# Infini-attention and a dense layer on one core: tile 1's V products ahead of wk's, and the order list searched again

## The chip, the core and the metric

One Trainium2 chip, one core of it. The time is microseconds of the device for one execution of the whole program. Engines are named as in the profile: PE (matrix products), DVE (vector), ACT (activations), POOL (GpSimd), SP (the queue from which nearly all transfers are issued). PSUM is the memory into which PE writes; the kernel uses eight banks of it, 512 float32 columns each.

## What is computed

`xn` is the layer norm of `x` (2048 rows of 512, bfloat16). Two things are added to `x`:

```python
# A: 32 heads of 16, four segments of 512 rows; M and z start at 0
p = softmax(q_s @ k_s.T / 4 + mask); a_dot = p @ v_s
a_mem = (phi(q_s) @ M) / (phi(q_s) @ z + 1e-6)       # phi(t) = t + 1 if t > 0 else exp(t)
o_s = sigmoid(beta) * a_mem + (1 - sigmoid(beta)) * a_dot
M, z = M + phi(k_s).T @ v_s, z + sum(phi(k_s))
# out = x + concat(o_s) @ wo + silu(xn @ w1) @ w2      (B: w1 is 512 x 1792)
```

`mask[i, j]` is -1e9 where i < j and 0 elsewhere.

## The kernel before

The work is cut into some 1349 small pieces, each a call of a short function, and one string, `ORDER` (from line 16, one line of it for each visit), lists them in the order in which they are issued. Every engine executes its own pieces in that order and waits for the others by semaphores alone. A launcher at the end of the kernel (line 895 on) reads the string word by word; `S0`, `h0.0.1`, `vv0.0` are such words: a piece's name and its numbers.

The segments (the first number of most words, s) have 512 rows, four tiles of 128. The words that the texts below use:

- `xs t` (L291; `xc`, `xd` its halves, L286 and L289): layer norm statistics of tile t on DVE; `xg`, `xq`, `xi` the inverse root; `Nv t` (L315): the normalised rows, on DVE.
- `X t.1` (L845): four transposes of tile t on PE, for tiles 0 to 3; `Xa`, `Xv` (L851) copy the result into xnT. Tiles from 4 on are turned by a transfer of SP (`XD t`, L857).
- `k s.dt.part`, `q`, `h`, `v s.tile.part` (L370, L395, L485, L401; through `product`, whose two forms are L336 and L338): a part of a product of xn with wk, wq, w1, wv. A part is one product of 512 columns in segments 0 and 1 (for k, q and h of segment 0 two of 256), two of 512 later on; four parts, later two, fill a PSUM bank.
- `kv`, `ka`, `qv`, `qa`, `vv`, `va` (L376, L399, L406): the finished bank is copied to SBUF, by DVE (`v` behind the name) or ACT (`a`). `kp`, `kf` (L385, L392, L393) make the keys' parity copies k3 from it.
- `ha` (L492), `hv` (L497): tanh on ACT, then the product on DVE, which frees the bank of h. `fp`, `fa`, `fv` (L417, L423, L433): phi of k, on POOL, ACT and DVE; `gp`, `ga`, `gv` of q.
- `S t` (L707 to L760): a visit. PE makes scores of four heads into psS, one tile of four banks (L724), ACT exponentiates all of it (L730), POOL masks (L744). There is one psS, so that the next visit's products wait for the exponential of the one before. Each exponential also waits for its place in ACT's order.
- `E n`, `O n` (L791): weights by V, even and odd heads; `Ev`, `Ov` (`Ea`, `Oa`) copy them out (L821, L828) and two transfers move the sums into zraw; `Om` (L835) merges.
- `s`, `sv`, `r`, `w` (`R`, `W` in the last segment): sums, their reciprocals and the gate; `z`, `d` (L577): transfers that spread them, `zv`, `dv` (L589, L599) the products; `n`, `nv` (L608): the memory's part; `t` (L441), `m`, `mv`, `mw` build the memory.
- `o s.tile.i` (also `oc`, `od`, `oh`: a half, a quarter, half a row): the last product, of hT with w2 for i up to 13 and of the attention with wo for 14 to 17; `st`, `sh` add x and store.

Two things bound the freedom of the list. PSUM: four banks are psS's, and the other four go round among k, q, v, h, E, O, n, m, s, X and o; a word that opens a bank waits until the copy of the bank's last content is done. And the array: a score product takes the array in row tiles, E and O in column tiles of 32, dense words either whole (L336) or in columns (L338), whichever suits the next S, E, O, s or m in the list; the launcher decides it so:

```python
        elif piece in ("k", "q", "v", "h", "n", "o", "oc", "od", "oh"):
            now = ahead[i] if now == "rows" else now
            now = "whole" if now == "rows" else now
        narrow[0] = now == "cols"
        PIECES[piece](*(int(n) for n in word[len(piece) :].split(".") if n))
```

Which of the four banks a word gets follows from the order, too: the pool hands out one that is free at that place of the list. The loads of x and of the weights stand ahead of the list, on SP's and ACT's queues: x tiles 0 to 3, wv, wk, wq, x tiles 4 to 7 (x_hi), w1, the rest of x. 50 products on zeros (`busy`) run while the first tile is normalised.

Of the kernel before, what the change touches and what calls it, by code (L numbers as in the profile page):

```python
# [25 lines left out]
S6 fa0.3 k1.2.0 k1.2.1 k1.2.2 h0.5.0 h0.5.1 h0.5.2 q1.1.0 h0.5.3 ha0.5 k1.2.3 kv1.2 q1.1.1 q1.1.2 hv0.5
S8 h0.7.0 q1.1.3 qv1.1 h0.6.0 h0.6.1 h0.6.2 h0.6.3 ha0.6 fv0.3 E1 Ev1 k1.0.0
S9 hv0.6 h0.7.1 h0.7.2 h0.7.3 Om0 ha0.7 k1.0.1 k1.0.2 kp1.2 q1.0.0 q1.0.1 q1.0.2 fp0.1 Nv9 XD9 xs12 k1.0.3 kv1.0 kp1.0
S10 h0.8.0 hv0.7 h0.8.1 h0.8.2 h0.8.3 ha0.8 h0.9.0 h0.9.1 q1.0.3 t0.3 Nv10 XD10 h0.9.2 h0.9.3 qv1.0
S13 hv0.8 O1 Ov1 xs15 v1.0.0 v1.0.1 v1.0.2 ha0.9 v1.0.3 vv1.0 h0.10.0 h0.10.1 bmask  # L30
S12 k1.1.0 k1.1.1 k1.1.2 t0.2 k1.1.3 kv1.1 h0.10.2 h0.10.3 ha0.10 hv0.9 h1.0.0 Om1 h1.0.1 h1.0.2
S15 h1.10.0 h1.10.1 h1.10.2 hv0.10 kp1.1 xl0.2 h1.0.3 ha1.0 Nv11 XD11 E2 Ev2 O2 Ov2
S17 h1.10.3 k1.3.0 hv1.0 k1.3.1 k1.3.2 k1.3.3 kv1.3 fp1.3 h0.12.0 h0.12.1 xs14 m0.2 mv0.2 ha1.10 h0.12.2
S21 fv0.1 q1.3.0 q1.3.1 q1.3.2 q1.3.3 qv1.3 h1.3.0 hv1.10 gp1.1 h0.12.3 ha0.12 t0.1 h1.3.1 h1.3.2 t0.0 h1.3.3
S14 hv0.12 k2.2.0 h0.11.0 h0.11.1 k2.2.1 h0.11.2 h0.11.3 xl0.0 h0.13.0 ha1.3
S16 ha0.11 h0.13.1 h0.13.2 kp1.3 h0.13.3 xs13 kv2.2 hv1.3 ha0.13 q2.1.0 q2.1.1 qv2.1 E3
S19 Ev3 h1.11.0 h1.11.1 h1.11.2 h1.11.3 hv0.11 O3 hv0.13 fa1.3 k2.1.0 mw0.2 k2.1.1 Ov3 kv2.1 Om2
S24 h1.8.0 h1.8.1 h1.8.2 h1.8.3 m0.0 mv0.0 q2.3.0 q2.3.1 qv2.3 ha1.8 hv1.8
S18 v2.1.0 v2.1.1 vv2.1 ga1.0 k2.0.0 o0.2.7 oc0.2.5.0 ha1.11 sv0 r0.1 o0.2.4 k2.0.1 kv2.0 xg12.4
S22 fv1.3 v2.2.0 v2.2.1 vv2.2 o0.2.1 ga1.1 gp1.2 o0.2.6 o0.0.3 o0.0.13 od0.2.11.1 hv1.11 r0.2 o0.0.10  # L40
S20 o0.2.0 oc0.0.2.0 r0.3 lw1 o0.2.2 od0.0.0.2 oc0.2.10.1 h1.1.0 h1.1.1 h1.1.2 h1.1.3 kp2.1 E4 r0.0 od0.0.0.1 ha1.1 gate w0 gv1.1 kp2.0 z0.1
S28 o0.0.6 hv1.1 z0.2 o0.0.8 z0.3 o0.0.11 o0.0.5 Ev4 oc0.0.7.1 Om3 z0.0 o0.2.8 o0.0.12 ga1.2 O4 Ov4
S26 q2.0.0 q2.0.1 h1.7.0 h1.7.1 h1.7.2 h1.7.3 gv1.2 ha1.7 qv2.0 oc0.2.10.0 od0.0.0.3 oc0.0.2.1
S23 fp1.2 od0.2.11.3 h1.4.0 hv1.7 h1.4.1 h1.4.2 Nv14 o0.2.12 h1.4.3 ha1.4 od0.2.11.0 oc0.0.7.0 zv0.3 h1.9.0 o0.2.13 h1.9.1
S25 h1.9.2 h1.9.3 ha1.9 Nv12 XD12 o0.2.3 oc0.2.5.1 gp1.0 zv0.2 o0.2.16 o0.0.16 hv1.4 zv0.0 XD14 zv0.1 E5 o0.0.17 Ev5 hv1.9
S29 fa1.2 o0.2.17 o0.2.14 k2.3.0 gv1.0 k2.3.1 kv2.3 h1.2.0 h1.2.1 h1.2.2
S27 o0.0.9 mw0.0 O5 o0.2.15 Ov5 o0.2.9 Nv13 fp1.0 XD13 h1.2.3 ha1.2 od0.2.11.2 fv1.2 st0.2 t1.2 o0.0.14 o0.0.15
S31 o0.0.4 h1.13.0 h1.13.1 h1.13.2 h1.13.3 ha1.13 o0.3.8 Om5 o0.3.11 o0.3.16 hv1.2 o0.3.9
S30 o0.3.14 h1.12.0 h1.12.1 h1.12.2 h1.12.3 t1.3 Nv15 hv1.13 ha1.12 XD15 od0.0.0.0 o0.1.16 od0.1.8.2 o0.1.17 o0.1.12 hv1.12 oc0.1.9.0
S33 o0.0.1 od0.1.8.3 o0.3.1 xl0.1 od0.1.8.0 st0.0 oc0.1.3.0 o0.1.13 oc0.1.3.1 xl0.3 gp1.3 Om4 fa1.0 o0.1.2 E6 o0.1.0  # L50
S32 kp2.3 Ev6 O6 Ov6 o0.3.17 o0.3.13 o0.3.10 o0.1.6 oc0.3.2.1 o0.1.15 m1.2 fa2.0 mv1.2 fv1.0
S35 o0.1.4 q2.2.0 q2.2.1 qv2.2 fp2.0 ga1.3 v2.0.0 v2.0.1
S34 h1.5.0 h1.5.1 o0.1.14 o0.1.11 t1.0 vv2.0 h1.5.2 oc0.3.0.1 xl1.0 gv1.3 fp1.1 h1.5.3 ha1.5 E7
S41 o0.1.7 Ev7 o0.3.12 o0.1.1 hv1.5 O7 v2.3.0 mw1.2 fa1.1 Ov7 v2.3.1 vv2.3 fv1.1 t1.1
S37 o0.3.5 q3.3.0 q3.3.1 Om7 qv3.3 od0.1.8.1 s1 o0.1.5 sv1 r1.2 o0.1.10 oc0.1.9.1 st0.1 r1.0 od0.3.3.2 ga2.3 kp2.2
S36 k3.1.0 k3.1.1 q3.1.0 q3.1.1 qv3.1 r1.3 r1.1 w1 d1.2 z1.1 z1.2 ka3.1 o0.3.4
S40 h1.6.0 h1.6.1 h1.6.2 h1.6.3 fp2.3 h2.8.0 h2.8.1 ha1.6 o0.3.7
S43 oc0.3.0.0 o0.3.6 od0.3.3.0 hv1.6 od0.3.3.1 m1.0 mv1.0 oc0.3.2.0 od0.3.3.3 o0.3.15 st0.3 o1.2.8 ha2.8 o1.2.7 hv2.8 fv2.0 E8 Ev8 gp2.3
S38 o1.2.13 fa2.2 v3.0.0 v3.0.1 Om6 k3.0.0 od1.2.1.1 k3.0.1
S42 kv3.0 o1.2.6 o1.2.2 o1.2.10 d1.1 h2.11.0 h2.11.1 ha2.11 o1.2.0 t2.0 vv3.0 zv1.1 gv2.3 o1.2.4 fp2.2 zv1.2  # L60
S39 hv2.11 q3.2.0 ga2.1 q3.2.1 qv3.2 d1.0 v3.3.0 v3.3.1 va3.3 E9
S44 dv1.2 q3.0.0 q3.0.1 Ev9 mw1.0 oc1.2.3.1 oc1.2.11.1 od1.2.1.3 fv2.2 gp2.2 n1.2 d1.3 O8 nv1.2 fa2.3 Ov8 xl1.2 oc1.2.3.0
S45 oc1.2.11.0 o1.2.9 h2.7.0 h2.7.1 ha2.7 qv3.0 fv2.3 v3.2.0 v3.2.1 vv3.2
S48 hv2.7 h2.6.0 h2.6.1 ha2.6 k3.2.0 k3.2.1 z1.3 dv1.3 o1.0.4 dv1.0 kv3.2 ga2.2 o1.0.0 oc1.0.7.1
S47 od1.0.1.3 hv2.6 h2.0.0 od1.2.1.2 h2.0.1 ha2.0 dv1.1 zv1.3 t2.2 n1.3 Om8 o1.0.6 o1.2.5 o1.0.16 nv1.3 hv2.0 gp2.1 o1.0.13
# [877 lines left out]
```

## Time and profile before

| what | value |
|---|---|
| three runs | 220.78, 219.94, 220.15 us; median 220.15 |
| the profiled execution | 219.96 us, of which its span is 218.2 us |
| PE, ACT, DVE, POOL busy | 210.9, 184.1, 181.3, 127.4 us |
| granted clock of PE | 1.00 |
| exponentials | 72, 1.88 us each, the first at 12.4, the last at 190.4 us |
| wk's load | issued at 2.68, on the chain that ended last for 5.81 us |
| last product on PE | starts at 215.0 us |

A line of the timeline gives the start, the duration, the engine, the line of the code, the operation and the tiles (out<-in); in square brackets stands the time that the engine stood idle before it, and what ended that. "x10" says that ten instructions in a row were merged. The windows give each engine's busy time in a stretch. Where a busy engine is named as the bound, its pace has to be looked at, since a busy PE can be one that waits inside.

### The profile page before, as it was taken

To read this page: it belongs to the slowest core of one execution; us is meant where nothing else is said; L and a number is where in the kernel's file an instruction comes from. 1 tells how busy PE (TensorE), PEld (TensorE's weight loads), DVE (VectorE), ACT (ScalarE), POOL (GpSimd) and SP (SyncE) were. 2 spreads that over 40 slices of the span, in tenths; PEclk is the share of its full clock that TensorE was granted. 3 is DMA by queue.
4 is the path that set the end of the run, shared out by engine and by line. 5 is a ranking of instruction groups with operands and counts; after the bars stand their busy time and mean duration, and the time that the engine had idled before them with its cause. 6 is when DMAs were issued, how large, how long until landed. Compare 5 with 4: busy or idle time off the path is not lost.

```text
span 218.2 us, 9267 instructions
## 1 busy us (share of the span) xinstructions
PE 210.9 (97%) x3982; PEld 116.1 (53%) x4006; DVE 181.3 (83%) x370; ACT 184.1 (84%) x173; POOL 127.4 (58%) x203
## 2 busy tenths in 40 slices
...
PEclk9999999999999999999999999999999999999999
...
DMA packets 33273, 19.60 MB, mean 90 GB/s; under 512 B 14672, under 2 KB 33232, under 8 KB 33232
## 3 DMA queue, kind: packets, MB, share of 16 engines
...
q8 instruction: 31, 0.51, 1.0%
...
## 4 chain that ended last, share of the span: by engine, by line
PE 92%; DMA 3%; ACT 2%; issue 1%; SPq 1%; DVE 0%
PE ps L336 26%; PE psO L338 17%; PE ps L338 16%; PE psS L724 11%; PE psO L336 9%; PE psV L791 8%; PE psS L338 4%; DMA wk_sb<-in_A_wk_dram 3%; ACT Pb L730 2%; PE psM L452 1%; SPq L169 0%; SPq L158 0%; PE ps L509 0%; ACT th L492 0%; DVE o_half L668 0%
## 5 line engine op out<-in xcount | busy, mean ns | idle before, releaser
L730 ACT ACTIVATE Pb<-psS 128x2048 bf16<-128x2048 f32 x72 | 135.2, 1878 | 4.7 <-PE psS L724 2.4
L744 POOL TENSOR_SCALAR_AFFINE_SELECT Pb<-Pb 128x512 bf16<-128x512 bf16 (+2 forms) x88 | 62.3, 718 | 22.4 <-ACT Pb L730 19.6
L497 DVE SCALAR_TENSOR_TENSOR hT<-th,ps 128x512 bf16<-128x512 bf16 x56 | 38.0, 682 | 10.1 <-ACT th L492 9.4
L744 POOL TENSOR_SCALAR_AFFINE_SELECT lows<-Pb 64x512 bf16<-64x512 bf16 (+1 forms) x40 | 24.3, 607 | 32.0 <-ACT Pb L730 24.9
L338 PE MATMUL psO<-w_sb,hT 128*32 128x512 bf16 (+2 forms) x696 | 41.4, 321 | 0.0
L336 PE MATMUL ps<-xnT,w_sb 128*128 128x512 bf16 (+1 forms) x177 | 35.9, 330 | 0.2 <-issue 0.2
L492 ACT ACTIVATE th<-ps 128x512 bf16<-128x512 f32 x56 | 33.0, 594 | 3.5 <-PE ps L338 3.1
L338 PEld LDWEIGHTS <-hT 128*32 128x32 bf16 x864 | 21.5, 96 | 14.6 <-issue 3.1
L338 PE MATMUL ps<-xnT,w_sb 128*32 128x512 bf16 (+1 forms) x408 | 24.8, 349 | 0.0
L724 PE MATMUL psS<-qT,k 32*128 32x64 bf16 (+3 forms) x512 | 23.0, 233 | 0.2
L336 PEld LDWEIGHTS <-w_sb 128*128 128x128 bf16 x178 | 16.4, 98 | 11.9 <-issue 1.2
L336 PE MATMUL psO<-w_sb,hT 128*128 128x512 bf16 (+2 forms) x82 | 20.5, 324 | 0.7 <-issue 0.6
L791 PEld LDWEIGHTS <-Vz 128*32 128x32 bf16 x768 | 16.1, 97 | 9.5 <-issue 0.6
L791 PE MATMUL psV<-Pb,Vz 128*32 128x448 bf16 (+7 forms) x512 | 21.0, 286 | 0.0
L724 PEld LDWEIGHTS <-k 32*128 32x128 bf16 x512 | 9.3, 92 | 21.2 <-issue 20.4
L336 PE MATMUL ps<-xnT,wk_sb 128*128 128x256 bf16 (+1 forms) x63 | 14.4, 326 | 0.4 <-DMA wk_sb<-in_A_wk_dram 0.2
L724 PE MATMUL psS<-qT,kT 16*128 16x448 bf16 (+3 forms) x256 | 14.7, 269 | 0.0
L338 PEld LDWEIGHTS <-w_sb 128*32 128x32 bf16 x408 | 10.3, 96 | 6.7 <-issue 1.7
L621 DVE SCALAR_TENSOR_TENSOR o_out<-psO,x_res 128x512 bf16<-128x512 f32 x14 | 9.4, 679 | 5.0 <-PE psO L338 3.9
L336 PEld LDWEIGHTS <-hT 128*128 128x128 bf16 x92 | 8.5, 98 | 9.6 <-issue 2.1
L828 DVE CAST odd<-psV 128x512 bf16<-128x512 f32 x16 | 11.0, 687 | 2.4 <-PE psV L791 2.4
L338 PE MATMUL psO<-wo_sb,oT 128*32 128x512 bf16 x140 | 12.8, 379 | 0.0
...
## 6 DMA issues: line engine op xcount, KB each, us to landing
...
```

Source lines behind the costliest of these rows:

```text
L336: return [nc.tensor.matmul(out, lhsT=lhsT, rhs=rhs, start=start, stop=stop, skip_group_check=True)]
L338: nc.tensor.matmul(out[c : c + 32], lhsT=lhsT[:, c : c + 32], rhs=rhs, start=start, stop=stop, tile_position=(0, c), skip_group_check=True,)
L452: nc.tensor.matmul(psM[32 * g : 32 * g + 32, i, :].rearrange("p (r d) -> p r d", d=DH), lhsT=st["phiK", dt][:, j, 32 * g : 32 * g + 32], r ...
L492: nc.scalar.activation(out=th[:], in_=sts[s]["h", ft][:, :], func=AF.Tanh, scale=0.5)
L497: nc.vector.scalar_tensor_tensor(out=st["hT"][:, ft, :], in0=st.pop(("th", ft))[:], scalar=1.0, in1=st.pop(("h", ft))[:, :], op0=ALU.add, ...
L621: out = nc.vector.scalar_tensor_tensor(out=o_out[:], in0=st.pop(("psO", j)), scalar=0.5, in1=st["x", j][:], op0=ALU.mult, op1=ALU.add)
L724: nc.tensor.matmul(psS[:, g, c : c + q2 - q1], lhsT=keys[rows], rhs=st["qT"][rows, dt, q1:q2], start=True, stop=True, tile_position=(32 * ...
L730: exp = nc.scalar.activation(out=blocks(Pb, b).rearrange("p y g c -> p g y c"), in_=psS[:, :, :].rearrange("p g (y c) -> p g y c", c=BLOCK ...
L744: over[id(Pb)].append(nc.gpsimd.affine_select(out=out, in_=in_, compare_op=ALU.is_ge, fill=0.0, base=base, pattern=[[0, out.shape[1]], [1, ...
L791: nc.tensor.matmul(psV[32 * g : 32 * g + 32, q0 : q0 + nq].rearrange("p (y c) -> p y c", y=weights.shape[2]), lhsT=Vzs[s % 2][:, kt, 4 * d ...
L828: copy(out=odd[:], in_=sts[s].pop(("psV", 1))[:, :])
```

## The change

Nothing but the string `ORDER` is changed. The set of pieces is the same but for nine copies, which go to the other of DVE and ACT. Ahead of S0, wk's product k0.1.0 gives its place, between the transposes X2 and X3, to v0.1.0, and v0.1.1 follows X3; words of the dense products around the first visits stand earlier or later; and from there on the whole list has another order, the order of the visits excepted. From the diff, the head, the first visits, and the lines that the prediction names:

```diff
-ones0 ones1 zeros xc0 xd0 xc1 xq0 xi0 Nv0 busy44 xd1 xq1 xc2 busy6 xi1 X0.1 xd2 xq2 Nv1 X1.1 Xa0.1 v0.0.0 v0.0.1 v0.0.2 xs3 xi2 Nv2 xq3 xi3 v0.0.3 X2.1 Xa1.1 k0.1.0 tb Nv3 X3.1 Xv2.1 k0.1.1 Xv3.1 vv0.0 odd omask k0.0.0 k0.0.1 k0.0.2 k0.0.3 ka0.0 fp0.0 q0.0.0 kf0.0 q0.0.1 q0.0.2 q0.0.3 k0.1.2 k0.1.3 q0.2.0 v0.2.0 qa0.0 xs5 ka0.1 kp0.1
-S0 v0.1.0 v0.1.1 xs6 xs7 q0.2.1 v0.2.1 v0.2.2 v0.2.3 vv0.2 fa0.0 k0.2.0 k0.2.1 k0.2.2 xs4 xg4.4
-S2 q0.2.2 q0.2.3 qv0.2 k0.2.3 kv0.2 fp0.2 fa0.2 v0.1.2 v0.1.3 vv0.1 Nv5 Nv6 XD6 q0.1.0 q0.1.1 q0.1.2 q0.1.3 qv0.1
-S1 h0.0.0 h0.0.1 h0.0.2 xs10 h0.0.3 v0.3.0 v0.3.1 v0.3.2 v0.3.3 ha0.0 vv0.3 q0.3.0 kp0.2 hv0.0
-S3 h0.3.0 h0.3.1 q0.3.1 q0.3.2 h0.3.2 tanh XD5 h0.3.3 k0.3.0 Nv7 XD7 q0.3.3 qv0.3 k0.3.1 xs8 ha0.3
-S4 Nv4 h0.1.0 k0.3.2 h0.1.1 hv0.3 XD4 h0.2.0 h0.2.1 h0.2.2 h0.2.3 ha0.2 xs9 k0.3.3 kv0.3 hv0.2
...
+ones0 ones1 zeros xc0 xd0 xc1 xq0 xi0 Nv0 busy44 busy6 X0.1 xd1 xq1 xc2 xi1 xd2 xq2 Nv1 X1.1 Xa0.1 v0.0.0 v0.0.1 xs3 v0.0.2 xi2 Nv2 v0.0.3 xq3 xi3 Nv3 Xa1.1 X2.1 Xv2.1 v0.1.0 X3.1 Xv3.1 v0.1.1 tb k0.0.0 k0.0.1 vv0.0 k0.0.2 odd k0.0.3 ka0.0 kf0.0 fp0.0 k0.1.0 xs5 q0.0.0 q0.0.1 q0.0.2 q0.0.3 qa0.0 k0.1.1 k0.1.2 k0.1.3 kv0.1 kp0.1 xs7 fa0.0
+S0 xs4 v0.2.0 v0.2.1 v0.2.2 v0.2.3 v0.1.2 xs6 xg4.4 k0.2.0 k0.2.1 va0.2 k0.2.2 k0.2.3 kv0.2 fp0.2
+S2 q0.1.0 q0.1.1 v0.1.3 vv0.1 fa0.2 q0.1.2 q0.1.3 qv0.1 q0.2.0 q0.2.1 q0.2.2 q0.2.3 qv0.2
+S1 q0.3.0 q0.3.1 Nv6 XD6 h0.0.0 Nv7 h0.0.1 h0.0.2 h0.3.0 h0.0.3 h0.2.0 ha0.0 fv0.2 xs9 hv0.0 q0.3.2
+S3 h0.3.1 h0.3.2 h0.2.1 h0.2.2 h0.3.3 ha0.3 Nv5 q0.3.3 fp0.1 tanh qv0.3 k0.3.0 k0.3.1
+S4 k0.3.2 k0.3.3 hv0.3 v0.3.0 XD7 kv0.3 kp0.3 v0.3.1 Nv4 h0.2.3 ha0.2 h0.1.0 v0.3.2 v0.3.3 vv0.3 h0.1.1
+S7 kp0.2 xs11 h0.1.2 h0.1.3 ha0.1 XD5 v1.2.0 v1.2.1 v1.2.2 v1.2.3 XD4 E0 hv0.2
+S5 v1.1.0 v1.1.1 v1.1.2 v1.1.3 vv1.2 Ev0 xl0.2 h0.4.0 h0.4.1 h0.4.2 h0.4.3 ha0.4 h0.5.0 hv0.1 xs8 xs10 hv0.4 xg8.4
+S11 v1.3.0 v1.3.1 h0.5.1 h0.5.2 omask vv1.1 h0.5.3 v1.3.2 v1.3.3 vv1.3 O0 Ov0 fa0.1 lw0
+S6 ha0.5 fv0.1 q1.2.0 q1.2.1 q1.2.2 q1.2.3 fa0.3 Nv9 Nv10 k1.2.0 k1.2.1 qv1.2 q1.1.0 q1.1.1 q1.1.2 q1.1.3 XD9 qv1.1
+S8 XD10 h0.6.0 h0.6.1 h0.6.2 h0.6.3 hv0.5 fp0.3 xs13 k1.2.2 k1.2.3 kv1.2 ha0.6 h0.8.0 h0.8.1 E1 Ev1
...
+S16 h0.13.1 h0.13.2 h0.13.3 Om2 ha0.11 q2.1.0 q2.1.1 t0.0 Nv12 kp1.2 qv2.1 E3 Ev3 ha0.13 hv0.13
+S19 Om0 Nv14 XD14 h1.11.0 h1.11.1 h1.11.2 h1.11.3 ha1.11 O3 Ov3 q2.3.0 kp1.3 q2.3.1 hv0.11 qv2.3
+S24 h1.8.0 hv1.11 gate h1.8.1 h1.8.2 h1.8.3 ha1.8 k2.1.0 k2.1.1 o0.2.7 kv2.1 kp2.1
...
+S46 hv2.0 oc1.0.10.0 h2.12.0 o1.0.0 zv1.0 d1.1 dv1.1 h2.12.1 ha2.12 O9 dv1.0 o1.2.17 Ov9
...
+S62 d2.3 o2.0.7 od2.0.6.2 o2.0.8 o2.2.3 n2.0 nv2.0 xl2.2 o2.0.11 z2.1 od2.2.13.2 zv2.3 oc2.2.6.0 o2.0.9 ga3.0 E13 Ev13 gv3.1
+S63 h3.4.0 h3.4.1 ha3.4 o2.2.10 O13 oc2.0.5.1 Om9 o2.2.12 mw2.0
+S67 Ov13 oc2.2.6.1 hv3.4 o2.2.0 o2.2.2 h3.8.0 dv2.3 gv3.0 h3.8.1 ha3.8 n2.3 nv2.3 o2.2.5 o2.2.14
...
+S65 o2.1.13 od2.1.9.2 o2.1.15 Om12 o2.1.2 o2.0.4 d2.2 dv2.2 o2.1.7 oc2.0.5.0 E14 Ea14 oc2.1.3.0 o2.0.15
...
```

The last line of the list, S71, holds in both kernels what is left of the output products, with the last segment's R, W, z, d and n between.

121 lines of the change are left out of this document (54 added, 67 removed).

## The prediction

> **What bounds the kernel now.** I read the page first, then the windows, the matrix products (PE) in the timeline, and the list word by word. The first two lines are the page's, the next the clock; below them the tile view's exponentials and five stretches of the windows (columns: PE, PEld, DVE, ACT, POOL busy, clock, DMA share, GB/s).
>
> ```profile
> span 218.2 us, 9267 instructions
> PE 210.9 (97%) x3982; PEld 116.1 (53%) x4006; DVE 181.3 (83%) x370; ACT 184.1 (84%) x173; POOL 127.4 (58%) x203
> PEclk9999999999999999999999999999999999999999
> ...
> L730 ACT ACTIVATE Pb<-psS x72: 1872/1877/1898, 12.4 to 190.4; 128x2048 bf16<-128x2048 f32 x72
> ...
> 0.00:10.00 10.00, 8.09 (x81) 6.87 (x82) 7.44 (x21) 5.21 (x12) 3.48 (x15) 1.00 0.79 254
> ...
> 20.00:30.00 10.00, 9.80 (x151) 6.36 (x154) 9.68 (x21) 9.95 (x10) 7.71 (x13) 1.00 0.27 48
> 30.00:40.00 10.00, 9.89 (x192) 6.03 (x186) 9.79 (x25) 9.70 (x10) 6.41 (x10) 1.00 0.81 209
> 40.00:50.00 10.00, 9.94 (x222) 5.77 (x225) 9.77 (x17) 9.86 (x9) 8.79 (x14) 1.00 0.35 74
> 50.00:60.00 10.00, 9.95 (x225) 5.74 (x222) 8.38 (x18) 9.90 (x10) 7.51 (x14) 1.00 0.19 44
> ```
>
> The profiled execution took 219.96 us: a span of 218.2 and 1.8 around it; it lies 0.19 under the median of the three runs, 220.15. PE is busy 97% of the span, and a busy PE could still be slow, so its pace comes next.
>
> ```profile
> 21.55 0.21 PE L724 MATMUL psS<-qT,k 32*128 32x64 bf16 x4
> ...
> 22.34 1.25 PE L336 MATMUL ps<-xnT,w_sb 128*128 128x256 bf16 x10
> 23.43 0.38 PE L336 MATMUL ps<-xnT,wk_sb 128*128 128x256 bf16 x2
> 23.93 0.40 PE L724 MATMUL psS<-qT,k 32*128 32x64 bf16 x8
> ...
> 186.35 1.03 PE L336 MATMUL ps<-xnT,w_sb 128*128 128x512 bf16 x4
> 187.31 0.40 PE L724 MATMUL psS<-qT,k 32*128 32x64 bf16 x8
> ```
>
> Ten products of 256 columns start from 22.34 until the next group at 23.43: 0.109 each. Four of 512 columns last 1.03, of which the last one's pipeline is 0.38: 0.216 apart. So one **unit** (a product of 512 columns, or two of 256) is 0.217 us, and PE runs at that pace. The fourth unit started at 187.00 and the next visit's first score product at 187.31: 0.31, which is 0.216 and 0.10 for the change of array mode. A visit is the stretch from one S word to the next. Here the two rows of S4 and S7, 21.55 and 23.93, are 2.38 apart, though the list gives that visit eight units and not nine; the last two products start at 23.43 and 23.54, and PE then stands idle from about 23.75 for some 0.19 until the exponential (1.88) has given psS back. That is the floor of a visit, 2.38 to 2.40; with nine units PE fills it exactly. Where the list has fuller visits, PE sets the time. So the time is: PE's start, its work, and what PE stands idle. Any idle time, wherever it falls, is paid in full.
>
> **The change, part by part.** *Work.* The two lists have the same 819 PE words; nine of the 1349 words differ, and only in whether ACT or DVE makes a copy. Counting modes as the launcher does, both have 144 changes of array mode. So PE's work differs by 0. The units after the last visit S71 fall by 1.56 us (the units counted at 0.217) and those before it rise by as much: moved, not saved.
>
> *Start.* Next come PE's rows, then ACT's, up to the first exponential.
>
> ```profile
> 7.91 0.40 PE L845 MATMUL ptr<-ident,xn_t 128*128 128x128 bf16 x4
> 8.54 0.39 PE L336 MATMUL ps<-xnT,wk_sb 128*128 128x256 bf16 x2 [0.24 <-DMA wk_sb<-in_A_wk_dram]
> 8.77 0.39 PE L845 MATMUL ptr<-ident,xn_t 128*128 128x128 bf16 x4
> 8.99 1.28 PE L336 MATMUL ps<-xnT,wk_sb 128*128 128x256 bf16 x10
> ...
> 11.95 0.21 PE L724 MATMUL psS<-qT,k 32*128 32x64 bf16 x4
> ...
> 7.59 0.62 ACT L851 COPY xnT<-ptr 128x256 bf16<-128x256 bf16 x2
> ...
> 10.30 0.58 ACT L376 CAST kT<-ps 128x512 bf16<-128x512 f32 x1 [0.58 <-PE ps L336]
> 10.92 0.51 ACT L393 ACTIVATE k<-kT,pm_even 128x256 bf16<-128x256 bf16 x1
> 11.34 0.56 ACT L399 CAST qT<-ps 128x512 bf16<-128x512 f32 x1
> 11.80 0.59 ACT L376 CAST kT<-ps 128x512 bf16<-128x512 f32 x1
> 12.40 1.88 ACT L730 ACTIVATE Pb<-psS 128x2048 bf16<-128x2048 f32 x1
> ```
>
> Transpose X2 starts at 7.91 and takes four steps of 0.056, so PE is free at 8.13; k0.1.0 starts at 8.54, when wk has landed: 0.41 idle. After, v0.1.0 runs at 8.13 (it reads the first half of tile 1's turned rows, the first of ACT's two copies from 7.59 to 8.21), X3.1 as soon as its row is normalised (8.42 by the row at 7.96 plus 0.41, in the last fence), v0.1.1 at 8.64, k0.0.0 at 8.86, past wk's landing. Twelve units then stand before S0: 8.86 + 12 x 0.217 + 0.10 = 11.56. But S0 also needs qa0.0. k0.0.3 ends at 8.86 + 7 x 0.109 + 0.27 = 9.90; ACT does ka0.0 (0.58) and kf0.0 and has room for qa0.0 0.42 after kf0.0 started, at 10.97; q0.0 ends at 10.99, so qa0.0 is done at 11.58 and S0 starts at 11.63, **0.32 earlier**. fa0.0, now ahead of S0 in ACT's queue, starts some 0.46 after qa0.0 and is out before S0's products (0.40) are through. It could cost 0.1, which S0's successor would show.
>
> *What is late next.* Line S3 opens k0.3 in a PSUM bank that h0.0 held; hv0.0 on DVE frees it. These are DVE's rows, the first of another window, the last two a later pair for the pace of fv.
>
> ```profile
> 7.96 0.41 DVE L315 TENSOR_SCALAR xn_t<-x_lo,mv_all,rstd_all 128x512 bf16<-128x512 bf16 x1
> ...
> 11.51 0.69 DVE L286 BATCH_NORM_STATS2 stats<-x_hi 128x6 f32<-128x512 bf16 x1 [0.23 <-DMA x_hi<-in_A_x_dram]
> ...
> 15.32 0.69 DVE L399 CAST qT<-ps 128x512 bf16<-128x512 f32 x1
> 15.93 0.68 DVE L376 CAST kT<-ps 128x512 bf16<-128x512 f32 x1
> ...
> 17.13 1.18 DVE L315 TENSOR_SCALAR xn_t<-x_hi,mv_all,rstd_all 128x512 bf16<-128x512 bf16 x2
> 18.22 0.68 DVE L399 CAST qT<-ps 128x512 bf16<-128x512 f32 x1
> 18.82 0.68 DVE L286 BATCH_NORM_STATS2 stats<-x_hi 128x6 f32<-128x512 bf16 x1
> ...
> 19.63 0.66 DVE L406 CAST Vz<-ps 128x512 bf16<-128x512 f32 x1
> 20.21 0.68 DVE L497 SCALAR_TENSOR_TENSOR hT<-th,ps 128x512 bf16<-128x512 bf16 x1
> ...
> 28.33 0.68 DVE L433 SCALAR_TENSOR_TENSOR pk<-ex,pos 128x512 bf16<-128x512 bf16 x1
> 28.94 0.69 DVE L406 CAST Vz<-ps 128x512 bf16<-128x512 f32 x1
> ```
>
> From start to start, a copy takes 0.60, a pair of norms 1.09, a statistics word (xs) 0.81 (18.82 to 19.63), fv 0.61. DVE's second stage begins at 11.51, when x_hi lands, and the change doesn't move that load. After, five xs (4.05), five copies (3.00), Nv6 and Nv7 (1.09) and fv0.2 (0.61) stand between 11.51 and hv0.0: it starts at 20.26, much as the 20.21 of before, and is through at 20.94. PE, however, comes sooner: S0 at 11.63 and three visits of 2.40 put S3 at 18.83; S3's own 0.40 and six units (1.30) bring k0.3.0 to 20.53. It waits until 20.99, then two units of k0.3 (0.44) and a mode change: S4 at 21.53, where before has 21.55. So **0.30 of the 0.32 is given back**. The bounds: 0 if DVE were done 0.46 sooner, 0.45 if x_hi lands 0.15 later.
>
> *The moves and the search.* Between S4 and S19, before ran from 21.55 to the start of its twentieth visit; after lists there for DVE one more hv, vv and Ev (3 x 0.60), one xs (0.81), two Nv (1.09), a small omask, and one fv fewer: 3.1 us more. DVE's free time in the windows from 20 to 60 is 0.32 + 0.21 + 0.23 + 1.62 = 2.4. So DVE is 0.7 short in that stretch, over a queue that was already behind. Where a bank hangs on it, PE waits: h0.6.0 (line S8) needs qv1.2. From hv0.0 on, 13 copies and hv, one fv, three xs and four Nv (13.0 us) end qv1.2 at about 34.0, or 34.4 with the waits for PE that I count; PE wants the bank at about 34.2 (S4 and five visits): 0 to 0.2, I take 0.1. h1.8.0 (line S24) needs Ov3, behind Om2, Nv12, qv2.1, Ev3, hv0.13, Om0 and Nv14: 0 to 0.7, the whole shortage; I take 0.2, since two thirds of it fall in words that no bank waits for. Later, n2.3 stands two words after dv2.3 (line S67), behind Om9, mw2.0, Ov13 and hv3.4: 0 to 0.5, I take 0, for the windows of before leave DVE more room there than in any line above. On SP the moved transposes, the moves to zraw and the spreads are issued in the list's order and by their own releases, so they run ahead of the list. d1.1 and d2.2 now stand one word ahead of their readers dv1.1 and dv2.2, but their buffers come free over fifty words earlier, so I count 0; if SP were late, DVE would stand still for the transfer. On POOL the nearest product to its visit's masking is O12, 2.9 us of PE units behind S57 (3.0 before): 0.
>
> **Sum:** -0.32 + 0.30 + 0.1 + 0.2 = +0.3. On the profiled 219.96 that is 220.25, on the median 220.45; I put the forecast at **220.4**.
>
> **Rivals.** (1) *The gain is kept*: k0.3.0 doesn't wait, and the ties hold. For it: before shows not one such wait after 9 us. Against: x_hi's row. 220.15 - 0.32 = 219.85. (2) *DVE becomes the bound of the first quarter*: each tie from S3 to S24 is missed and the shortage arrives whole, with n2.3's 0.5: -0.32 + 0.45 + 0.2 + 0.7 + 0.5 = +1.5, so 221.7, slower. It decides from the point where DVE has no idle slice between 11.5 and 60. For it: 9.68 to 9.79 of 10 busy already; against: a late PE gives DVE time, so waits don't all add. (3) *The moved V products do nothing*: S0 stays at 11.95, since qa0.0 or fa0.0 holds it. Then k0.3.0 waits only 0.14, which its visit's idle 0.19 covers: with the other terms 220.45, the same as the forecast to the eye. [...]
>
> **How the numbers follow.** Forecast, with rival 3, 0.58; rival 1 0.20; rival 2 0.17; rival 4 0.02; some saving that I don't see, over 1 us, 0.03. A measurement of this kernel tells about 0.5%, 1.1 us, from no change: faster means under 219.05, slower over 221.25. The forecast and rival 1 lie within (0.78, less 0.01 for the forecast's upper edge), rivals 2 and 4 beyond: faster 0.03, same 0.77, slower 0.20. The range goes from rival 1 less the runs' own spread (0.2 below their median) to 221.6, by rival 2.
>
> **What would show it.** S0 near 11.63 and no wait on wk ahead of PE; the group k0.3.0 about 20.99, some 0.4 late, and S4 near 21.5; hv0.0 near 20.3. If S4 comes by 21.3, the second step is wrong and rival 1 holds. PE waits of 0.1 to 0.5 ahead of h0.6 (near 34) and h1.8 (near 62), and DVE over 9.5 of 10 in the window from 50 to 60. I would be wrong altogether if PE stood idle over 1 us at one place that I passed over, the chain from the last exponential to nv3.3 above all, where the tail is now 1.56 shorter.

## The result, and the profile after

| | before | after |
|---|---|---|
| median | 220.26 us (16 executions, 219.89 to 221.09) | 221.34 us (16 executions, 220.15 to 222.15) |
| profiled execution, its span | 219.96, 218.2 | 222.04, 220.3 |
| S0's first product, S71's, the last on PE | 11.95, 189.99, 214.99 | 11.77, 192.12, 216.85 |

The ratio of the times is 1.004 (95% interval 1.0022 to 1.0059). The forecast was 220.4 with a range of 219.6 to 221.6; the loss over before is 1.08 where the forecast had 0.3. The profiled execution of after is one of its slowest, 0.7 above its median, so its waits are rather an upper case. The times spread by 2.0 us, before's by 1.2.

The page of the changed kernel, three lines. The last is a row of part 3: queue, packets, MB, share.

```profile
span 220.3 us, 9330 instructions
PE 211.4 (96%) x4011; PEld 115.5 (52%) x4036; DVE 179.2 (81%) x369; ACT 185.3 (84%) x174; POOL 124.6 (57%) x203
q8 instruction: 31, 0.51, 1.0%
```

Both lists have the same products, yet the page shows PE as 0.5 us busier: the end of a product is modelled, and a busy PE can be one that waits. So the page doesn't say where the 2.1 us of span go. The timeline does: PE's last product starts 1.86 later, and 0.22 more lie behind it. First the start (PE, its weight loads, ACT). Where PE waits, I give the wait as **product time**: the distance from one product's start to the next, less the step that the first of them takes. The idle time in a row differs from it, since that counts from a modelled end.

```profile
8.64 1.28 PE L336 MATMUL ps<-xnT,wk_sb 128*128 128x256 bf16 x10
...
10.05 0.77 PEld L336 LDWEIGHTS <-wq_sb 128*128 128x128 bf16 x8 [0.41 <-DMA wq_sb<-in_A_wq_dram]
10.05 1.05 PE L336 MATMUL ps<-xnT,wq_sb 128*128 128x256 bf16 x8
...
11.13 0.58 ACT L399 CAST qT<-ps 128x512 bf16<-128x512 f32 x1 [0.28 <-PE ps L336]
...
11.77 0.21 PE L724 MATMUL psS<-qT,k 32*128 32x64 bf16 x4
```

The wait for wk is gone: ten products run from 8.64 and their steps end at 9.73. Then PE stands still until wq lands, 0.30 of product time (10.05 less the last start, 9.64, less a step of 0.11), and S0 follows q0.0.0's start by 1.72: q0.0 (1.05), its copy (0.58) and what lies between. A wait for one load has become a wait for the next one.

The row of the stage of S1 to S4 that the second step of the prediction is about (DVE, then PE):

```profile
17.68 0.83 DVE L315 TENSOR_SCALAR xn_t<-x_hi,mv_all,rstd_all 128x512 bf16<-128x512 bf16 x2
...
19.86 0.66 DVE L497 SCALAR_TENSOR_TENSOR hT<-th,ps 128x512 bf16<-128x512 bf16 x1
...
20.62 0.60 PE L336 MATMUL ps<-xnT,wk_sb 128*128 128x256 bf16 x4
21.35 0.21 PE L724 MATMUL psS<-qT,k 32*128 32x64 bf16 x4
```

hv0.0 is through at 20.52, and k0.3.0, the first two of the four products at 20.62, doesn't wait for it. S4 comes at 21.35, 0.20 earlier than before. DVE's load in the windows of after (columns as in the prediction):

```profile
20.00:30.00 10.00, 9.75 (x162) 6.30 (x165) 9.45 (x20) 9.96 (x10) 7.99 (x14) 1.00 0.28 59
30.00:40.00 10.00, 9.89 (x196) 5.80 (x187) 9.65 (x20) 9.64 (x10) 5.92 (x10) 1.00 0.91 214
40.00:50.00 10.00, 9.94 (x230) 5.79 (x231) 9.15 (x22) 9.88 (x9) 8.13 (x13) 1.00 0.54 84
50.00:60.00 10.00, 9.95 (x227) 5.78 (x220) 9.43 (x21) 9.76 (x10) 7.21 (x13) 1.00 0.14 28
```

DVE is less busy than before up to 50 and 1.05 busier from 50 to 60: what was moved arrives there. The next waits lie in four visits. I found them by setting each visit's length, from S to S, against the work that the list gives it; for a visit without a wait, that difference is the same within 0.03 us in each profile. The rows of three of them:

```profile
65.04 0.84 DVE L521 TENSOR_SCALAR zsum<-zraw,evec 128x256 f32<-128x256 bf16 x1 [0.54 <-DMA zraw<-odd]
65.92 0.55 DVE L545 RECIPROCAL ri<-zsum 128x64 f32<-128x64 f32 x1
...
66.39 0.16 DVE L464 COPY M<-psM 128x64 f32<-128x64 f32 x1
...
66.61 0.81 PE L336 MATMUL ps<-wv_sb,xnT 128*128 128x512 bf16 x2 [0.34 <-DVE M L464]
...
100.31 0.61 POOL L417 TENSOR_SCALAR pos<-kT 128x512 bf16<-128x512 bf16 x1
100.88 0.65 POOL L744 TENSOR_SCALAR_AFFINE_SELECT Pb<-Pb 128x512 bf16<-128x512 bf16 x1
...
101.58 0.62 PE L791 MATMUL psV<-Pb,Vz 128*32 128x448 bf16 x16
...
115.52 0.69 POOL L385 TENSOR_SCALAR k<-kT,pm_odd 128x512 bf16<-128x512 bf16 x1
116.19 0.89 POOL L385 TENSOR_SCALAR k<-kT,pm_even 128x256 bf16<-128x256 bf16 x1
117.16 0.61 POOL L417 TENSOR_SCALAR pos<-kT 128x512 bf16<-128x512 bf16 x1
...
118.57 1.09 POOL L744 TENSOR_SCALAR_AFFINE_SELECT Pb<-Pb 128x1024 bf16<-128x1024 bf16 x1
...
119.71 0.28 PEld L791 LDWEIGHTS <-Vz 128*32 128x32 bf16 x11 [0.34 <-issue]
```

In S22, sv0 (L521) waits on DVE for a transfer, r0.1 follows it, and mv0.0 (L464), which gives back the bank of v2.2.0, is queued behind both: PE loses 0.39. In S41, POOL does fp1.1 (L417) before it masks S34's weights (100.88 to 101.53), and O7 starts at 101.58, 0.18 late; in S39, kp3.1 (L385) and fp2.0 stand ahead of S42's mask, and E9's main part starts at 119.71, when the mask ends: 0.24. In S21, h1.3.0 waits 0.16 for hv1.10, which stands behind xs12. Note that no row names POOL as a releaser at 101.58; the mask's end and the product's start lie 0.05 apart, and that the one releases the other is a guess until it is tried.

Then the tail, PE and DVE; behind it the chain of waits, which is told in start, duration, what.

```profile
204.94 0.43 DVE L589 TENSOR_TENSOR oT<-spr,oraw 128x512 bf16<-128x512 bf16 x1
...
205.40 0.69 DVE L608 TENSOR_TENSOR oT<-ps,oT 128x512 bf16<-128x512 f32 x1
...
206.14 0.40 PE L338 MATMUL ps<-phiQT,Mbf 128*32 128x512 bf16 x4 [0.24 <-DVE oT L608]
...
210.18 0.42 DVE L589 TENSOR_TENSOR oT<-spr,oraw 128x512 bf16<-128x512 bf16 x1 [1.10 <-DMA spr<-rz]
...
210.71 0.69 DVE L608 TENSOR_TENSOR oT<-ps,oT 128x512 bf16<-128x512 f32 x1
...
211.46 0.40 PE L338 MATMUL psO<-wo_sb,oT 128*32 128x512 bf16 x4 [0.70 <-DVE oT L608]
```

```profile
205.39 0.60 SPq L577
205.99 0.04 issue
206.03 4.05 DMA spr<-rz
```

The first wait (0.41 of product time) is n3.1, behind nv3.2; the second (0.87) is the first product that needs nv3.3. Ahead of nv3.3 stands zv3.3, and ahead of that the last spread, z3.3. It is issued at 205.39, when zv3.2 has given its buffer back, a microsecond after W1's end (204.37), and its second half lands 4.06 after its issue. The halves of all of before's spreads there take 2.09 to 2.15.

One more wait stands behind PE's last product, and it isn't PE's. The first line is of the same chain, the second DVE's:

```profile
212.47 3.54 DMA x_res<-in_A_x_dram
...
216.14 0.69 DVE L621 SCALAR_TENSOR_TENSOR o_out<-psS,x_res 128x512 bf16<-128x512 f32 x1 [0.17 <-DMA x_res<-in_A_x_dram]
```

The last load of x for the final sum takes 3.54 from its issue (2.04 in before), and DVE waits for it. From PE's last product to the end of the span it is 3.48 instead of 3.26: the 0.22.

### The profile page after: what moved, and what is told of

Same layout as the page of the kernel before. It is cut to its first block, busy times and chain, and to the rows that moved or that the text cites. A ratio compares the mean times of both kernels' runs of the same rounds, so it can differ in the third digit from the quotient of the medians.

```text
span 220.3 us, 9330 instructions
## 1 busy us (share of the span) xinstructions
PE 211.4 (96%) x4011; PEld 115.5 (52%) x4036; DVE 179.2 (81%) x369; ACT 185.3 (84%) x174; POOL 124.6 (57%) x203
## 5 line engine op out<-in xcount | busy, mean ns | idle before, releaser
L744 POOL TENSOR_SCALAR_AFFINE_SELECT Pb<-Pb 128x512 bf16<-128x512 bf16 (+2 forms) x88 | 61.4, 707 | 22.6 <-ACT Pb L730 19.7
L744 POOL TENSOR_SCALAR_AFFINE_SELECT lows<-Pb 64x512 bf16<-64x512 bf16 (+1 forms) x40 | 23.1, 576 | 37.0 <-ACT Pb L730 31.5
L338 PE MATMUL psO<-w_sb,hT 128*32 128x512 bf16 (+2 forms) x688 | 42.8, 324 | 0.0
L336 PE MATMUL ps<-xnT,w_sb 128*128 128x512 bf16 (+1 forms) x152 | 31.6, 329 | 0.4 <-issue 0.2
L338 PE MATMUL ps<-xnT,w_sb 128*32 128x512 bf16 (+1 forms) x500 | 29.1, 346 | 0.0
L336 PE MATMUL psO<-w_sb,hT 128*128 128x512 bf16 (+2 forms) x85 | 21.2, 319 | 0.6 <-issue 0.5
L791 PE MATMUL psV<-Pb,Vz 128*32 128x448 bf16 (+7 forms) x512 | 21.3, 286 | 0.0
L336 PEld LDWEIGHTS <-w_sb 128*128 128x128 bf16 x155 | 14.6, 98 | 11.7 <-issue 1.3
L338 PEld LDWEIGHTS <-w_sb 128*32 128x32 bf16 x500 | 12.5, 96 | 8.0 <-issue 1.4
L336 PE MATMUL ps<-xnT,wk_sb 128*128 128x512 bf16 (+1 forms) x69 | 14.1, 330 | 0.2 <-DVE z L468 0.2
L336 PE MATMUL ps<-xnT,wq_sb 128*128 128x256 bf16 (+1 forms) x61 | 12.8, 324 | 0.5 <-DVE zsum L531 0.2
L336 PEld LDWEIGHTS <-hT 128*128 128x128 bf16 x94 | 8.4, 98 | 9.0 <-issue 1.9
L406 DVE CAST Vz<-ps 128x512 bf16<-128x512 f32 x15 | 10.3, 686 | 2.6 <-PE ps L338 1.9
```

The costliest lines, as they stand in the source:

```text
L336: return [nc.tensor.matmul(out, lhsT=lhsT, rhs=rhs, start=start, stop=stop, skip_group_check=True)]
L338: nc.tensor.matmul(out[c : c + 32], lhsT=lhsT[:, c : c + 32], rhs=rhs, start=start, stop=stop, tile_position=(0, c), skip_group_check=True,)
L406: copy(out=Vzs[s % 2][:, j, :, 0:3:2, :], in_=sts[s].pop(("v", j))[:, :].rearrange("p (h r d) -> p h r d", r=2, d=DH),)
L744: over[id(Pb)].append(nc.gpsimd.affine_select(out=out, in_=in_, compare_op=ALU.is_ge, fill=0.0, base=base, pattern=[[0, out.shape[1]], [1, ...
L791: nc.tensor.matmul(psV[32 * g : 32 * g + 32, q0 : q0 + nq].rearrange("p (y c) -> p y c", y=weights.shape[2]), lhsT=Vzs[s % 2][:, kt, 4 * d ...
```

## The experiments

"Start" is S0's first product, "rest" the time from it to the last product on PE, both of the profiled execution. "Rest" leaves out what lies behind the last product: 3.44 to 3.58 in after, e0_again, e1_om14, g1_cover and h3_tail_only, where DVE waits for that last load, and 3.26 to 3.28 in all others. Ratios are to before on the same chip, which took 220.36 (e), 220.36 (f), 220.12 (g), 220.33 and 220.17 (h1 and h2, h3).

| kernel | median | ratio, 95% | start, rest | waits in the tail |
|---|---|---|---|---|
| before | 220.26 | | 11.95, 203.04 | none |
| after | 221.34 | 1.004, 1.0022 to 1.0059 | 11.77, 205.08 | 0.41, 0.87 |
| e0_again | 221.41 (one) | | 11.95, 204.25 | 0.40, 0.39 |
| e1_om14 | 220.98 | 1.0031, 1.0011 to 1.0051 | 12.07, 203.51 | none |
| e2_zfree | 221.27 | 1.0046, 1.0023 to 1.0069 | 11.78, 204.33 | 0.40 |
| e3_fetch_later | 221.57 | 1.0054, 1.0033 to 1.0076 | 12.49, 203.66 | 0.40 |
| f1_swap_only | 220.36 | 1.0002, 0.9977 to 1.0027 | 11.79, 203.18 | none |
| f2_mid | 222.27 | 1.0083, 1.0055 to 1.0112 | 11.94, 204.47 | 0.40 |
| f3_mid_tail | 221.29 | 1.0032, 1.0002 to 1.0062 | 11.91, 204.88 | 0.82 |
| g1_cover | 222.23 | 1.0086, 1.0054 to 1.0118 | 12.03, 205.27 | 0.79 |
| g2_all | 221.68 | 1.0071, 1.0045 to 1.0097 | 12.01, 204.54 | 0.79 |
| h1_single_moves | 219.91 | 0.9972, 0.9952 to 0.9992 | 11.91, 202.93 | none |
| h2_with_cover | 220.38 | 1.0002, 0.9986 to 1.0019 | 12.00, 203.25 | none |
| h3_tail_only | 221.16 | 1.0036, 1.0017 to 1.0054 | 12.29, 203.91 | none |

**The tail: a late issue, or a held-up transfer?** In the packet records of after, a fetch of 16 KB of instructions begins at 207.12, in the middle of z3.3's second half; the view of transfers shows it for 206.9 to 208.7:

```profile
q8 instruction: 1, 0.02, 5.3%
```

> The changed kernel unaltered, one more profile. Two theories of PE's wait of 0.87 us at 210.5 (first attention product after the last spread, z3.3). Theory A, the chain: z3.3 is issued only when zv3.2 has given its buffer back (205.39, a microsecond after W1), and that alone makes the wait; then it is there in each execution, 0.7 to 1.0. Theory B, the fetch: z3.3's last piece took 4.06 us from issue instead of 2.1 because a fetch of 16 KB of PE's own instructions (207.12, 1.53 us) was on one of the transfer's sixteen queues; then the wait comes and goes: about 0 where z3.3 lands within 2.3 us of issue, with a time of 220.2 to 221.1, and 0.7 or more with a time over 221.5 where it takes 3.5 or more. The wait of 0.41 at 205.5 (n3.1 behind nv3.2) is in both.

The unaltered kernel again. Its chain of waits has

```profile
205.87 3.57 DMA spr<-rz
```

and the wait at 210.3 is 0.39: the transfer was held up again, by 1.5 instead of 2.0, and the wait is smaller by 0.5. The first wait is 0.40. This fits B's lengths, not A's 0.7 to 1.0; that the hold-up can be absent altogether, it doesn't show.

```diff
-S71 ... Om13 o3.2.3 ... o3.0.11 Om14 z3.0 oh12.1 zv3.2 ...
+S71 ... Om13 Om14 o3.2.3 ... o3.0.11 z3.0 oh12.1 zv3.2 ...
```

> The changed kernel with the merge Om14 placed right behind Om13, where DVE has 0.40 us idle, instead of just ahead of zv3.2. Theory A: zv3.2 comes 0.45 earlier, so nv3.2 frees the bank of n3.1 earlier and the first wait of 0.41 goes; z3.3 is issued near 204.85 and the second wait shrinks by as much as the first gave back at most; median 220.6 to 221.0. Theory B: the first wait goes too, but PE's fetch comes 0.4 earlier with PE, so z3.3 is still hit in most executions: second wait 0.5 to 1.0, median 220.8 to 221.2. Rival C, the tail doesn't count in the median: no change, 221.3.

Both waits are gone, and the chain that ended last is PE alone:

```profile
by line: PE psO L338 41.0%; PE psS L338 30.6%; PE ps L338 4.1%; DVE o_half L668 2.0%; issue 0.1%
```

zv3.2 starts at 204.43, z3.3's halves are issued at 204.88 and 205.53, and land 2.10 behind. The fetch begins at 206.74 and meets the load of x_res instead (3.26). The median is 0.36 under the changed kernel's, but the intervals of the two ratios overlap, so a gain in the median isn't shown.

```diff
-        to = work.tile([P, L], BF16, name="spr", bufs=4)
+        tag = "pk" if s == LAST and k == 0 else "spr"
+        to = work.tile([P, L], BF16, name="spr", tag=tag, bufs=4)
```

> The changed kernel with the last segment's four z spreads in a set of buffers of their own (that of the keys' phi products, free by then), so that none waits for dv3 or zv3. Issues: z3.2 near 200.05, z3.1 and z3.0 right behind it, z3.3 near 204.4 (W1's end), 1.0 earlier. Theory A: the second wait, 0.87, goes altogether, the first, 0.41, stays: median 220.3 to 220.6. Theory B: z3.3's pieces are through by about 207.1, just as the fetch starts, so the wait goes in most executions: 220.4 to 220.8; where the fetch still meets it, z3.3 takes 3.5 or more from issue. Rival C: 221.3.

z3.3 is issued at 204.54, 0.85 earlier, lands in 2.10, and the second wait is gone; the first stays at 0.40. The fetch begins at 207.36, after z3.3 has landed, so this run doesn't tell the late issue from the fetch. The median is the 221.3 of rival C.

```diff
-            nc.tensor.matmul(idle[:, 0:P], lhsT=zraw[:, 0:P], rhs=zraw[:, 0:P], ...)
+            nc.tensor.matmul(idle, lhsT=zbig[:, 0:P], rhs=zbig[:, :], ...)
-... Nv0 busy44 busy6 X0.1 ...
+... Nv0 busy18 X0.1 ...
```

> The changed kernel with the 50 products on zeros of 128 columns at the start replaced by 18 of 512 columns (another tile of zeros): the same time on PE (about 3.9 us) with 64 instructions fewer, so that every fetch of PE's instructions comes a quarter of a block, about 1.5 us, later against the work, and the list is untouched. Theory B: the fetch that met z3.3 comes near 208.6, z3.3 lands within 2.3 us of issue, the second wait is under 0.15; median 220.3 to 220.8, and the spread of the times is smaller. Theory A: nothing changes, z3.3 is issued at 205.4 and PE waits 0.7 to 0.9; median 221.3. If the start suffers from the other zeros, the first exponential shows it (12.22 before).

The list is as in after, z3.3 is issued just as late (205.58, 206.22), and no wait is left behind n3.1's (L591 is the changed kernel's L589):

```profile
205.58 1.25 SPq L579 DMA_DIRECT2D spr<-rz  x2
...
209.19 0.42 DVE L591 TENSOR_TENSOR oT<-spr,oraw 128x512 bf16<-128x512 bf16 x1
```

The fetch begins at 209.19 instead of 207.12, and z3.3 lands in 2.10. So Theory A alone falls, as far as one profile can show it: the late issue took away the room, and the fetch made the wait. B's other half fails: the median didn't fall. In this profile S0 comes at 12.49, since wq landed at 10.72; whether the other zeros do that, one profile can't say. So how much the fetch costs in the median is open.

**The start alone**, in the kernel before:

```diff
-... X2.1 Xa1.1 k0.1.0 tb Nv3 X3.1 Xv2.1 k0.1.1 Xv3.1 ... q0.0.3 k0.1.2 k0.1.3 q0.2.0 v0.2.0 qa0.0 ...
-S0 v0.1.0 v0.1.1 xs6 xs7 ...
+... X2.1 Xa1.1 v0.1.0 tb Nv3 X3.1 Xv2.1 v0.1.1 Xv3.1 ... q0.0.3 k0.1.0 k0.1.1 k0.1.2 k0.1.3 qa0.0 ...
+S0 q0.2.0 v0.2.0 xs6 xs7 ...
```

> The kernel before with one part of the change alone: v0.1.0 and v0.1.1 take the places of k0.1.0 and k0.1.1 at the start, these two go ahead of k0.1.2, and q0.2.0 and v0.2.0 go behind S0, so that S0 has as many units ahead of it as before. My prediction's first step: S0 0.32 earlier. Theory W (wq's landing): with wk's wait gone, q0.0.0 waits for wq, which lands near 10.0 in each run; S0 comes 1.72 behind q0.0's start, near 11.75: 0.1 to 0.2 earlier, and PE stands idle 0.2 to 0.35 ahead of q0.0. The later visits keep their lengths of before, so that the last product starts 0 to 0.2 earlier; median 220.1 to 220.4 where before has 220.3. Rival G (given back): a wait for a bank or for POOL appears in a visit from S4 to S24 that has none in before, and takes it back there.

```profile
9.94 1.04 PE L336 MATMUL ps<-xnT,wq_sb 128*128 128x256 bf16 x8
...
11.79 0.21 PE L724 MATMUL psS<-qT,k 32*128 32x64 bf16 x4
...
14.31 0.40 PE L724 MATMUL psS<-qT,k 32*128 32x64 bf16 x8
```

q0.0.0 starts 0.05 after wq landed (9.89), and S0 is 0.16 earlier than before. S0's own visit is then 2.52 long instead of 2.39, so that 0.04 is left, and by S21 0.01. The last product starts at 214.97 (before: 214.99) and the time is the same within 0.3%. The swap by itself shows no gain; the 1.08 comes with the rest of the list.

**The middle.** Each suspected queue was changed: fp1.1 and fp2.0 go behind the visits whose masks they delayed, sv0 and r0.1 behind vv2.1, xs12 and xg12.4 behind mv0.2.

```diff
-S18 ... hv1.8 sv0 r0.1 oc0.2.5.1 ... v2.1.1 vv2.1 oc0.2.5.0
+S18 ... hv1.8 oc0.2.5.1 ... v2.1.1 vv2.1 sv0 r0.1 oc0.2.5.0
-S35 ... o0.1.10 fp1.1 gv1.3
+S35 ... o0.1.10 gv1.3
-S34 ... oc0.3.0.0
+S34 ... oc0.3.0.0 fp1.1
-S38 ... hv2.8 fp2.0 Om7 ...
+S38 ... hv2.8 Om7 ...
-S42 ... xl1.2
+S42 ... xl1.2 fp2.0
-S17 ... kv1.3 xs12 xg12.4 m0.2 ha1.10 hv1.10 mv0.2
+S17 ... kv1.3 m0.2 ha1.10 hv1.10 mv0.2 xs12 xg12.4
```

> The changed kernel with four moves in the middle, one for each visit that is longer than its work: fp1.1 behind S34 and fp2.0 behind S42 (POOL then masks those visits first), sv0 and r0.1 behind vv2.1, xs12 and xg12.4 behind mv0.2. If the masks are what O7 and E9 wait for, visits S41 and S39 get shorter by 0.18 and 0.24; if DVE's queue is what v2.2.0 and h1.3.0 wait for, S22 gets shorter by 0 or 0.39 (that wait is not there in each execution) and S21 by 0.15. Sum 0.57 to 0.96 at S71, tail unaltered: median 220.5 to 221.0. Rival: another wait takes their place in the next visits, and S71 stays where its work puts it, within 0.2 of the changed kernel: 221.3.

The length of each visit, in us:

| kernel | S21 | S22 | S41 | S39 | S14 | S19 | S44 |
|---|---|---|---|---|---|---|---|
| after | 2.54 | 3.00 | 2.59 | 3.00 | 2.39 | 2.73 | 2.40 |
| f2_mid | 2.38 | 2.61 | 2.40 | 2.77 | 2.65 | 3.04 | 3.04 |
| h1_single_moves | 2.50 | 2.61 | 2.40 | 2.77 | 2.39 | 2.74 | 2.40 |

The four visits got shorter by 0.16, 0.39, 0.19 and 0.23. For POOL's two the cause is shown: over all profiles S41 takes 2.58 to 2.60 and S39 2.85 to 3.02 in the seven with the changed kernel's order there, 2.40 and 2.77 in the five with a move. S22 is 2.61 in all five with sv0's move, but also in three of the seven without it, and 3.00 or 3.01 in the other four; that the move mends it is likely, not shown. S21 lies between 2.38 and 2.55 in the ten without its move, so its 2.38 here shows nothing. But three others got longer by 0.26, 0.31 and 0.64, and the median rose. These are the words that I had pushed back, and their readers. Two rows of f3_mid_tail, which has the same moves:

```profile
54.48 0.49 DVE L315 TENSOR_SCALAR xn_t<-x_end,mv_all,rstd_all 128x512 bf16<-128x512 bf16 x1 [0.85 <-POOL rstd_all L300]
...
120.01 0.93 DVE L433 SCALAR_TENSOR_TENSOR pk<-ex,pos 128x512 bf16<-128x512 bf16 x1 [0.73 <-POOL pos L417]
```

Nv13 waits for the root that xg12.4 has POOL make, and fv2.0 for fp2.0, each with DVE's queue behind it.

f3_mid_tail is these moves with that of e1_om14.

> The four moves of the middle and Om14 behind Om13 together. If both losses are as seen, the last product starts at most 203.3 us after S0 (before: 203.04; changed: 205.08 in its profile) and the median is 220.0 to 220.6, no different from before. If it stays above 220.9, something else than these waits costs time in the changed kernel: the end behind the last product, or the start.

The time is well over the expected one: the new waits stay, and the tail's second wait is back, 0.82, with Om14 where it was harmless in e1_om14. z3.3's second half was issued at 205.92 and took 4.10; the fetch began 1.18 after its issue (in after 1.09, in e0_again 1.11; in e1_om14, where it wasn't held up, 1.21).

**More room in the tail.** Is it the tail's 1.56 us that is missing?

```diff
-S66 ... o2.3.16 oc2.3.2.0 oc2.3.2.1 st2.0 ...
+S66 ... o2.3.16 st2.0 ...
-S69 o2.3.13 od2.1.9.1 ... od2.1.9.3 o2.3.15 h3.2.0 ... o2.1.4 o2.3.0 ha3.0
+S69 od2.1.9.1 ... od2.1.9.3 h3.2.0 ... o2.1.4 ha3.0
-S70 ... o2.1.8 o2.3.7 hv3.3 o2.1.17 O14 Oa14 o2.3.12
+S70 ... o2.1.8 hv3.3 o2.1.17 O14 Oa14
-S71 ... oh3.0 o2.3.3 n3.1 ...
+S71 ... oh3.0 o2.3.3 oc2.3.2.0 oc2.3.2.1 o2.3.13 o2.3.15 o2.3.0 o2.3.7 o2.3.12 n3.1 ...
```

> The changed kernel with six units of segment 2's output products (oc2.3.2.0, oc2.3.2.1, o2.3.13, o2.3.15, o2.3.0, o2.3.7, o2.3.12: 1.30 us) taken from the lines S66, S69 and S70 to just ahead of n3.1, behind the last visit: the tail of S71 then has nearly the units that it has before the change (1.56 more), and the chain from the last exponential to nv3.3 starts 1.30 earlier against PE. Theory R (the reserve of the tail is what was lost): both waits of the tail go, 0.40 and 0 to 0.87, whatever the fetch does, unless it costs z3.3 more than 1.5; the last product starts 0.4 to 1.3 earlier than in the changed kernel against S0 (204.25 to 205.08 there, 203.6 to 203.9 here); median 220.5 to 221.0. Rival Q (a queue: Om14 and W1 ahead of zv3.2 on DVE, whatever stands beside): a wait of 0.3 or more stays ahead of n3.1 or of the product behind it; median 221.2 or more. Visits S66, S69, S70 get 0.22, 0.65, 0.43 shorter in both.

```profile
187.62 1.02 PE L336 MATMUL ps<-xnT,w_sb 128*128 128x512 bf16 x4 [0.37 <-DVE o_out L621]
...
206.27 0.43 DVE L589 TENSOR_TENSOR oT<-spr,oraw 128x512 bf16<-128x512 bf16 x1 [1.77 <-PE psO L338]
```

Not a clean test. zv3.2 writes into oT, of which there is one, and o2.3.15 still had to read segment 2's: zv3.2 stands until it is through, and n3.1 waits 0.79. In S69, h3.0.0 now comes before its bank is free (0.53).

g2_all is that with Om14's move, two of the four moves of the middle (fp1.1; sv0 and r0.1), and for E9 another one: kp3.1 goes from S38 to S45.

> All that helped, in one kernel, without the two moves that made new waits: the tail's cover as in g1_cover, Om14 behind Om13, fp1.1 behind S34, sv0 and r0.1 behind vv2.1, and for E9 the keys' copies kp3.1 moved from S38 to S45, so that POOL masks S42 at once. Expected: S41 shorter by 0.18, S39 by 0.24, S22 by 0 to 0.39, no new wait, none in the tail; the last product 203.0 to 203.4 after S0 (before: 203.04); median 220.1 to 220.6, as before the change or 0.2 under it. If a fresh wait of over 0.2 comes up, each engine's queue is so full that a move mends one place and breaks another, and the loss can't be had back by single moves: 220.8 or more.

The middle is mended, with 0.13 left in S45: up to S59, where both lists have put the same work behind PE, before needs until 161.65, the changed kernel until 162.21 and this one until 161.68. The tail has g1_cover's waits.

**What helped, together**: fp1.1, sv0 and r0.1, Om14, the buffers, and kp3.1 in S53, where POOL has room.

> The changed kernel with all moves that took a wait away and made none: fp1.1 behind S34, sv0 and r0.1 behind vv2.1, Om14 behind Om13, the z spreads of the last segment in buffers of their own; kp3.1 goes to S53, where POOL has 1.7 us idle, instead of S45. Expected: the middle as in g2_all (S41, S39, S22 without a wait) and S45 at 2.38; no wait of over 0.15 in the tail if z3.3, issued at W1's end, is through before a fetch meets it; the last product 203.0 to 203.4 after S0 (before: 203.04), median within 0.3 of the kernel before. If the median stays 0.8 or more above before although the last product comes at most 203.4 after S0, the loss lies ahead of S0 or behind the last product.

Two lines of its page, and the first of its chain of waits from 198 on:

```profile
span 218.1 us, 9326 instructions
PE 211.4 (97%) x4011; PEld 116.6 (53%) x4036; DVE 178.7 (82%) x369; ACT 185.2 (85%) x174; POOL 124.8 (57%) x203
```

```profile
by line: PE psO L338 38.8%; PE psS L338 28.5%; PE ps L338 7.5%; DVE o_half L669 1.8%; issue 0.1%
```

No PE wait of over 0.13 is left behind S4, the chain is PE's, z3.3 lands in 2.10 (the next fetch begins 2.44 after its issue, when it is through), and the spread of the times is 1.2 again. It is faster than before by 0.28% (interval 0.08 to 0.48) and some 1.4 us faster than the changed kernel; the intervals of these two are apart. Since the work is the same, the changed kernel's loss was in waits that its order makes.

> h1_single_moves and a smaller cover of the tail, without the products that made g1_cover's waits: oc2.3.2.0, oc2.3.2.1 (line S66), o2.3.7 and o2.3.12 (S70), 0.65 us together, go to just ahead of n3.1; none of them reads segment 2's attention sums, whose only buffer zv3.2 overwrites, and S69 keeps its units. S66 and S70 get 0.22 and 0.43 shorter, no wait ahead of n3.1. If the tail's reserve still counts after Om14 and the buffers, the median is 0.1 to 0.4 under that of h1; if not, the two are the same within 0.2.

Not faster: no tail wait was left to cover, S69 is 0.10 longer, and S45 has its 0.13 again. So once Om14 and the buffers are mended, a longer tail isn't what is missing.

> Of h1_single_moves the two edits of the tail alone: Om14 behind Om13, and the z spreads of the last segment in buffers of their own; the middle is the changed kernel's. No wait of over 0.15 behind S71. S41 and S39 keep their 0.18 and 0.24, S22 its 0 to 0.39. The last product 203.4 to 203.9 after S0 (204.25 to 205.08 in the changed kernel, 202.93 in h1_single_moves); median 220.3 to 220.8, that is 0.4 to 0.9 over h1_single_moves and 0.5 to 1.0 under the changed kernel's 221.34. If it is the same as h1_single_moves (219.9), the middle's waits cost nothing in the median; if it stays at 221, the tail's do.

No wait of PE in the tail, the middle's three are there (S22 3.01, S41 2.60, S39 3.02), and the median, 221.16, is 0.4 above the upper end of what I expected. It is 0.18 under the changed kernel's, with nearly the same interval: by the test that I had set, the tail's waits cost little in the median. Some of it may lie at the ends: in this profile S0 comes at 12.29, the last load of x takes 3.71, and 3.58 lie behind PE's last product. h1_single_moves differs in the middle alone, and here the intervals are apart: 1.25 in the median, 1.36 in the last product of the two profiles, of which 0.38 is S0's, 0.85 the three visits', and 0.20 a wait in S55 that I didn't look into, less 0.07 in S21.

## Why the prediction held, and where it didn't

The sign held, and so did the account at large: PE's work is the same, and the start's gain is more than given back to waits. The size was off by 0.8, and that the median lies in the range is in good part luck. No term of the sum came out with its size at its place, and the two that I had put at nothing, POOL and the tail, are most of the loss in the profile, whose own 222.04 lies outside the range.

1. *S0 0.32 earlier*: 0.18 in the profile, 0.16 in f1_swap_only. The step let q0.0.0 start at about 9.95 because PE would be free, and didn't ask when wq lands; before had no wait there, so the load wasn't in sight. wq landed at 9.69 to 10.72 in the fourteen profiles. In the thirteen with the swap, S0 came at 11.77 to 12.49 (the middle one 11.95): against the 11.95 of before's one profile, no gain that can be counted on.
2. *0.30 given back at k0.3.0*: no wait. The term that was mis-sized is DVE's queue ahead of hv0.0: 8.75 forecast, 8.35 measured, mainly because the pair Nv6 and Nv7 took 0.76 to the next word, and not the 1.09 of the row that I had taken. S4 at 21.35 is close to the 21.3 that I had named as the sign against the step. The gain wasn't kept, though, as rival 1 has it: by S24 0.05 of it was left, after S22 none, and in f1_swap_only 0.01 at S21.
3. *0.1 at h0.6.0, 0.2 at h1.8.0*: none at either place. DVE's queue made PE wait at S21 (0.16) and S22 (0.39, in four of the seven profiles with that order): 0.55 where 0.3 stood, and my choice of the words that would miss was wrong. S22's isn't in my list at all: a word that waits for a transfer was moved ahead of one that frees a bank. I had listed for DVE what is queued, but not what each queued word waits for.
4. *POOL 0*: 0.42, confirmed by f2_mid. I measured the distance from a visit to its product in PE's units and took the nearest. What counts is the end of the mask, and that depends on what POOL was given ahead of it.
5. *Tail 0*: 1.28 and 0.79 in the two profiles of this kernel. This is the place that I had named for being wrong altogether. The reason given there, 1.56 us of units moved to the front, isn't needed for a wait to go: h1_single_moves keeps them in front and has none. Whether they would have covered the waits behind the last visit, no run shows, since g1_cover made new ones. What the runs show is the order on DVE (Om14 just ahead of zv3.2) and the spread's buffer, and for the second wait the fetch on top. In the medians, the tail's part isn't shown: e1_om14 and h3_tail_only lie 0.36 and 0.18 under the changed kernel, and the intervals overlap. The 0.22 behind the last product, a load again, is in no term of mine.
6. *The other rivals*. The time is nearer to rival 2's 221.7 than to the forecast, but not by its way: k0.3.0, h0.6.0, h1.8.0 and n2.3 show no wait, and DVE has idle time in each window from 20 to 60. Rival 3, S0 held at 11.95 by qa0.0 or fa0.0: S0 does follow qa0.0, but what holds qa0.0 is wq's load. Rival 4, which had 0.02, was a drop of PE's clock: the granted clock is 0.998 to 1.00 in each run of the changed kernel and its variants, and in the profile of after the middle step between two products of 512 columns is 0.216 (128x512, L336), as in before.
